# Scaling the attention values and taking some weight remainders on GpSimd, shifting three tiles' bits on VectorE, and moving one rounding forward

## The chip, the cores and the metric

The kernel runs on one core of one Trainium2 chip. The metric is the device time of one execution in microseconds (us); lower is better. Before the change the median of three runs is 564.09 us (562.98 to 564.4).

## What is computed

A retention layer (attention with a decaying state) over 2 batches of 8 heads, 768 positions and 64 channels, then two dense blocks on the 1536 x 512 result. Cut to what matters:

```
for t in range(S):                                   # retention, per batch and head
    state = gamma * state + outer(k[t], v[t])
    y[t] = scale * q[t] @ state
x = y as (1536, 512)
h = x @ w_in   (512 x 2048);  x = softplus(h) @ w_out        (2048 x 512)
h = x @ w2_in;                x = (h * clip(h + 3, 0, 6) / 6) @ w2_out
```

q, k and v are 32-bit numbers. The weights of both blocks reach the kernel as 64-bit numbers, two 32-bit words each, and the kernel itself turns them into 32-bit numbers.

## The kernel before, in words

**Names.** TensorE is PE, VectorE is DVE, ScalarE is ACT, GpSimd is POOL, SyncE is SP. A *unit* is 128 positions of one batch: there are 12, numbered 0 to 11. Units 0 to 3 make the first 512 rows of x and are the *head* of the kernel; units 4 to 11 are worked in pairs between the matmuls of the first dense block. A *weight tile* of the first block is 128 x 512 numbers: in0 to in15 from w_in, out0 to out15 from w_out. They are made in the order in0, in1, in2, out0, in3, out1, in4, out2, ... and numbered 0 to 31 in that order.

**Precision.** Each dense product is done three times in a rounded float32 form: high x high, high x low, low x high. So each weight tile, and each activation, is split: ACT copies it to the rounded *high* part, and the remainder, value minus high, is the *low* part.

**A weight tile** goes through these steps (class Words and weight()): SP loads its words into a `raw` buffer (five of them); ACT takes the top three bits of the low word (`bits`) and the sign (`sign`) into a `cv` buffer; the high word is scaled and clamped (`scale` on ACT and `clamp` on DVE, or `scaled` and `capped` on DVE); DVE joins them (`merge`); ACT rounds to the high part (`high`); DVE subtracts for the low part (`low`). For five tiles of the 32 the low part is made another way: ACT writes the negative and a DMA issued by POOL adds the value to it.

**A unit** loads k, q and v, turns k and q on PE (`ident` in the rows), scales q (`qT`) and v (`vs`) on DVE by powers of the decay, and multiplies: the scores, the masked scores with `vs`, and the state update with `vs`. In the head, the unit's result is rounded by ACT (`x_hi`) and the remainder is taken by DVE (`x_lo`). PE's first dense matmul needs `x_hi` of all four head units.

**The order.** Nothing is scheduled at run time. A planner (class Plan) holds every task with its engine, a cost, the tasks it follows and a due time, and hands out tasks greedily; the order in which it hands them out is each engine's program. Within a small window (NEAR) the task with the earliest due time goes first; a task with `ahead` set may be taken that much before it is ready. So a change of one task's engine or cost can re-order all engines. A GEMM block G1(f) is 12 matmuls of 128 x 512 with weight tile in f, G2(f) the same with out f on the softplus of G1(f)'s result.

**Pools.** `g2` holds five buffers for values that are read back from memory for the last 512 rows of the first block.

Of the kernel before, what the change touches and what calls it, by code (L numbers as in the profile page):

```python
# [10 lines left out]
F32 = mybir.dt.float32  # L11
F32R = mybir.dt.float32r
# [4 lines left out]
ALU = mybir.AluOpType  # L17
PSUM = bass.MemoryType.PSUM
P = 128
# [119 lines left out]
PSX, TT, TS, ACP, ACS = 0.61, 0.62, 0.36, 0.49, 0.55  # L139
# [6 lines left out]
def kernel(ctx, tc, q, k, v, w1_in, w1_out, w2_in, w2_out, table, out):  # L146
    nc = Plan(tc)
# [8 lines left out]
    CH = 512  # L156
    NC = NT // CH
    START = CH // C
    NU = B * NCH
    LAG = 2  # L160
    EARLY = 3
# [13 lines left out]
    def BY_DVE(n):  # L175
        return n < 10 or n < 2 * NF and n % 4 != 0
# [3 lines left out]
    def BY_ACT(n):  # L180
        return n < 4 or n >= 16

    def DIRECT(n):
        return True

# [16 lines left out]
    hold = holds.enter_context(tc.tile_pool(name="hold", bufs=1))  # L202

    def room(name, n, shape, dtype, within=None, later=()):
        nc.pool(name, n, later)
        slots[name] = {i: (within or fixed).tile(shape, dtype, name=f"{name}_{i}") for i in range(n)}
        kinds[name] = shape, dtype

    def at_slot(key):
        name, i = nc.slot[key]  # L210
        if name == "bank":
            return banks[:, i, :]
        if i not in slots[name]:
            slots[name][i] = late_p.tile(*kinds[name], name=f"{name}_{i}")
        return slots[name][i]
# [28 lines left out]
    room("g", 3, [P, CH], F32)  # L244
    room("hi", 2, [P, CH], F32R)
    room("lo", 3, [P, CH], F32R)
    for name, n, shape, dtype in (("sums", 1, [P, 4, CH // 2], F32), ("wf", 1, [P, 2, CH], F32), ("xl", 7, [P, 2, 2, CH], F32R), ("hs", 3, [P, CH], F32), ("g2", 5, [P, CH], F32), ("hi2", 7, [P, CH], F32R), ("lo2", 7, [P, CH], F32R),
                                  ("basel", 4, [P, CH], F32), ("partl", 2, [P, CH], F32), ("totall", 1, [P, CH], F32), ("xf", 7, [P, 2, 2, QT], F32R), ("keep", START + 2, [P, CH], F32), ("tf0", 2, [P, 2, QT], F32), ("tf1", 2, [P, 2, QT], F32), ("tf2", 2, [P, 2, QT], F32),
                                  ("base", 1, [P, QT], F32), ("part", 2, [P, QT], F32), ("total", 1, [P, QT], F32),
                                  ("c", 2, [P, 2, QT], F32), ("ob", 4, [P, CH], F32), ("e2", 2, [P, 2, QT], F32), ("parts", 3, [P, 2, 2, QT], F32R)):  # L250
        nc.pool(name, n)
        slots[name], kinds[name] = {}, (shape, dtype)
# [45 lines left out]
    n = 0  # L298
# [25 lines left out]
    for i in range(len(STEPS)):  # L324
        for name, n in PRODUCTS.items():
            n = min(n, 1) if i == 0 else n
# [10 lines left out]
    begin = -100.0  # L337
# [4 lines left out]
    def w_part(key, i):  # L342
        return at_slot(("w", key))[:, i]
# [7 lines left out]
    class Words:  # L351
# [26 lines left out]
        def bits(self):  # L378
            nc.scalar.activation(self.w(), self.raw()[:, :, 0], AF.Relu, scale=2.0 ** -29 * (1 - 2.0 ** -12), bias=half)

        def sign(self):
            nc.scalar.activation(self.w().bitcast(F16).rearrange("p (n x) -> p n x", x=2)[:, :, 1], self.y().bitcast(I32), AF.Copy, scale=2.0 ** -100)

# [12 lines left out]
        def merge(self):  # L396
            nc.vector.scalar_tensor_tensor(self.w(), self.y(), 3, self.w(), ALU.logical_shift_left, ALU.bitwise_or)

        def made(self, at, fetch_at, load, give, by_act=False, hold=0.0):
            T["F", self.key] = t0 = nc.add("SP", 0.45, self.fetch, due=fetch_at, take=[(f"raw{self.m}", self.raw_k)], load=load, hold=hold)  # L400
            t1 = nc.add("ACT", 0.65, self.bits, [t0], at - 3.5, take=[(f"cv{self.m}", self.cv_k)])
            if self.m or by_act:
                t4 = nc.add("ACT", SIGN, self.sign, [t1], at - 3.3)
                t2 = nc.add("ACT", 0.57, self.scale, [t4], at - 2.6)
                t3 = nc.add("DVE", TS, self.clamp, [t2], at - 2.0)
            else:
                t4 = nc.add("ACT", SIGN, self.sign, [t1], at - 2.9)
                t3 = nc.add("DVE", TS, self.scaled, [t0, t4], at - 2.7)
                t3 = nc.add("DVE", TS, self.capped, [t3], at - 2.3)
            return nc.add("DVE", TT, self.merge, [t3, t4], at - 1.3, give=give)  # L410

    def weight(o, f, number):
        key = 0, o, f
        x = Words(0, key, words[0][o])
        use = due[("G2" if o else "G1"), f] - 4.0
        made = second

        def high():
            nc.scalar.activation(w_part(key, 0), x.w().bitcast(F32), AF.Copy)

        def negative():
            nc.scalar.activation(w_part(key, 1), x.w().bitcast(F32), AF.Copy, scale=-1.0)

        def low():
            nc.vector.tensor_tensor(w_part(key, 1), x.w().bitcast(F32), w_part(key, 0).bitcast(F32), ALU.subtract)

        def add():
            nc.gpsimd.dma_start(out=w_part(key, 1).bitcast(F32), in_=x.w().bitcast(F32), accum_op=ALU.add)

        part = [("w", ("w", key))]  # L430
        tail = 1.5 if BY_DVE(number) else 7.0
        t5 = x.made(use - tail, begin + 15 if number < 1 else use - tail - 8.0, 1.45 if o else 1.5 if number < EARLY else 1.75, [x.raw_k], BY_ACT(number))
        if BY_DVE(number):
            a = nc.add("ACT", ACS, high, [t5], use - 1.5, take=part, give=[x.cv_k] + made)
            b = nc.add("DVE", TT, low, [a], use - 0.7, give=[x.cv_k] + made)
        else:
            n = nc.add("ACT", ACS, negative, [t5], use - tail, take=part)
            b = nc.add("POOL", 0.9, add, [n], use - tail + 1, give=[x.cv_k] + made, load=1.6)
            a = nc.add("ACT", ACS, high, [n], use - 2.5, give=[x.cv_k] + made)
        T["W", key] = [a, b]  # L440
        if not o:
            home = homes["in", f] = kept(f"words_in{f}", CH)
            T["S", key] = nc.add("SP", 0.45, lambda: nc.sync.dma_start(out=home, in_=x.w().bitcast(F32)), [t5], use, give=[x.cv_k] + made, load=0.8)
        elif o and f >= KEPT:
            home = kept(f"parts_out{f}")
            c = nc.add("SP", 0.45, lambda: nc.sync.dma_start(out=home, in_=at_slot(("w", key)).rearrange("p a n -> p (a n)").bitcast(F32)), [a, b], use + 8.0,
                       give=[("w", key)], load=1.6)
            for c_of in range(1 + (f in STAY), 3):
                back(("wl", c_of, f), home, c, due["G2", c_of * NF + f] - 8.0, 2.0)
# [4 lines left out]
    def kept(name, n=2 * CH):  # L454
        return stash.tile([P, n], F32, name=name)
# [19 lines left out]
    def back(key, home, after, when, lead=10.0):  # L475
        T["W", key] = [nc.add("SP", 0.45, lambda: nc.sync.dma_start(out=at_slot(key).rearrange("p a n -> p (a n)").bitcast(F32), in_=home),
                              [after], when, take=[("w", key)], load=1.6, hold=HOLD + when - lead)]
# [75 lines left out]
    for i, key in enumerate(order):  # L553
        weight(*key[1:], i)
# [64 lines left out]
    def attend(u):  # L619
        b, i = divmod(u, NCH)  # L620
# [5 lines left out]
        def task(eng, cost, fn, after, when, take=(), give=(), load=0.0, hold=0.0):  # L626
            when -= EDGE * (u < START and eng in ("DVE", "ACT"))
            return nc.add(eng, cost, fn, after, when, [(p, k) for p, k in take], list(give) + mine, load, hold)

        def tile_of(n):  # L630
            return at_slot((n, u))

        def own(n):
            return [(f"{n}{ph}", (n, u))]
# [17 lines left out]
        if u < START:  # L652
            at = [begin + 10 * u, begin + 10 * u + 1, begin + 10 * u + 3]
        else:
            at = [d["Tk"] - 11.0 + x / 2 for x in range(3)]
# [21 lines left out]
        sc, ds, o = ([(n, j, u) for j in range(2)] for n in ("sc", "ds", "o"))  # L677
        S, E = ("S", "D") if u < START else ("SS", "DD")
        kt, qt = [], []
        for x in range(parts):  # L680
            at = x and 0.1
            tp = task("PE", cost["Tk"] / parts, turned("k", x), [ik[x], ready.get(("S", u - 2))], d["Tk"] + at, take=[] if x else [("bank", ("kP", u))])
            kt.append(task("ACT", ACP if parts == 1 else act(NP * C // parts, True), lambda x=x: nc.scalar.activation(tile_of("kT")[:, ps(x)], bank(("kP", u))[:, ps(x)], AF.Copy), [tp], d[S] - 1.0 + at,
                           take=[] if x else own("kT"), give=[("kP", u)]))
            tp = task("PE", cost["Tq"] / parts, turned("q", x), [iq[x], ready.get(("C", u - 2))], d["Tq"] + at, take=[] if x else [("bank", ("qP", u))], give=[("q", u)])
            qt.append(task("DVE", PSX if parts == 1 else dve(NP * C // parts), lambda x=x: nc.vector.tensor_tensor(tile_of("qT")[:, ps(x)], bank(("qP", u))[:, ps(x)], tq_sb[:, ps(x)], ALU.mult), [tp, ready["q"]],
                           d[S] - 1.1 + at, take=[] if x else own("qT"), give=[("qP", u)]))
        vs = task("DVE", TT, lambda: nc.vector.tensor_tensor(
            tile_of("vs"), tile_of("v"), tk_sb.rearrange("p (h o) -> p h o", o=1).to_broadcast([P, H, HALF]), ALU.mult),
            [iv, ready["t"]], d[E] - 1.2, take=own("vs"), give=[("v", u)])  # L690
        if u >= START:
# [58 lines left out]
        if first:  # L750
            ready["end", u] = task("DVE", 0.42, faded, [dp, ready["t"]], (due["C", u + 1] if u + 1 < START else due["CC", u + 1]) - 2.0, take=[end], give=[end[1], dk])
            n = None
        else:
# [3 lines left out]
            n = task("DVE", 0.1, between, [c], d["C"] + 0.5)  # L757
        c = task("PE", cost["I0"], inner, pt + [vs, n], d["I"], take=[("bank", y) for y in o] if first else [],
                 give=[("pw", u), ("vs", u)])
        def x_at(part):  # L760
# [3 lines left out]
        o2 = task("ACT", PSX, lambda: nc.scalar.activation(x_at("hi"), split_out(), AF.Copy), [c], need - 1.5, give=o)  # L764
        o3 = task("DVE", PSX, lambda: nc.vector.tensor_tensor(x_at("lo"), split_out(), x_at("hi").bitcast(F32), ALU.subtract), [o2],
                  need - 0.8, give=o)
        ready["x", u] = [o2, o3]

    def pair(u, task):
# [479 lines left out]
```

## Time and profile before

| what | before |
|---|---|
| median of three runs | 564.09 us |
| the profiled execution's own time | 565.54 us |
| its span, first to last instruction | 563.4 us |
| granted TensorE clock | 1.0 of full speed throughout |
| PE busy | 554.1 us (98%) |
| DVE busy | 443.2 us (79%) |
| ACT busy | 365.3 us (65%) |
| POOL busy | 5.6 us (1%) |

The span is one execution by the hardware profiler; 2.1 us of the execution's own time lie around it. Line numbers are of little use, since a helper (L45) records nearly every operation: rows are told apart by engine and tile names, `output<-inputs`. Ends of matmuls are modelled, so a stall of PE shows best as a longer step between the starts of two matmuls.

### The profile page before, as it was taken

The page shows a single profiled execution, that of the slowest core. Times are in us where ns is not written, and L with a number is a line of the kernel's source. Part 1 is how long each engine was busy: PE and PEld are TensorE (multiplying, and loading weights), DVE is VectorE, ACT ScalarE, POOL GpSimd, SP SyncE. Part 2 cuts the span into 40 slices and gives each one's busy share as a digit, 9 for nine tenths or more (in the row PEclk, how much of TensorE's full clock was granted, in tenths as well). Part 3 has the DMA queues.
Part 4 walks back from the last instruction along what each step waited for, and adds up shares of the span by engine and source line. Part 5 has one row for each costly group of instructions (what it writes and reads, how often), then busy time and mean ns, then how long its engine had stood idle before and what let it go on. Part 6 is the DMA issues. An engine that isn't in the chain of part 4 may idle for free.

```text
span 563.4 us, 9586 instructions
## 1 busy us (share of the span) xinstructions
PE 554.1 (98%) x3679; PEld 473.3 (84%) x3679; DVE 443.2 (79%) x797; ACT 365.3 (65%) x604; POOL 5.6 (1%) x13
## 2 busy tenths in 40 slices
PE   8899999999999999999999999999999999999996
PEld 6688888787788888878888999988988899988895
DVE  4999998889989689989996885847787888854443
ACT  3598999998864445777957944448688685432220
POOL 0000000000000000000000000000000000000000
PEclk9999999999999999999999999999999999999999
DMA  9996999994423224846928522252655742236003
GB/s 204 282 247 244 284 281 290 340 281 165 139 64 105 94 77 152 276 169 224 328 88 293 187 74 76 74 188 76 229 212 194 269 180 76 75 100 237 1 0 113
DMA packets 80541, 98.41 MB, mean 175 GB/s; under 512 B 41328, under 2 KB 57968, under 8 KB 80496
## 3 DMA queue, kind: packets, MB, share of 16 engines
q1 hardware_dynamic: 79488, 96.35, 52.9%
q0 software_dynamic: 720, 1.31, 1.3%
q8 instruction: 29, 0.48, 0.4%
q10 hardware_dynamic: 288, 0.14, 0.1%
q14 instruction: 16, 0.13, 0.1%
HBM read 72.36 MB, written 24.12 MB: 171 GB/s over the span
## 4 chain that ended last, share of the span: by engine, by line
PE 74%; DVE 8%; ACT 7%; DMA 5%; issue 4%; POOL 0%; DVEq 0%; POOLq 0%; ACTq 0%; SPq 0%
PE banks L45 74%; ACT cv L45 3%; DMA w<-cv 1%; DMA raw<-in_moe_w_out_dram 1%; DVE w L45 1%; DVE raw L45 1%; ACT w L45 1%; DMA g<-stash_h 1%; DVE qT L45 1%; ACT raw L45 1%; DMA wf<-words_in 1%; DVE st L45 1%; DVE g L45 1%; DVE lo L45 1%; DVE cv L45 1%
## 5 line engine op out<-in xcount | busy, mean ns | idle before, releaser
L45 PE MATMUL banks<-w,parts 128*128 128x512 f32 x579 | 136.7, 390 | 0.0
L45 PEld LDWEIGHTS banks<-w,parts 128*128 128x128 f32 x579 | 108.1, 188 | 21.2
L45 PE MATMUL banks<-hi,w 128*128 128x512 f32 x384 | 125.1, 394 | 0.0
L45 PE MATMUL banks<-xf,w 128*128 128x384 f32 x672 | 123.6, 337 | 0.0
L45 PEld LDWEIGHTS banks<-xf,w 128*128 128x128 f32 x672 | 118.2, 188 | 3.5 <-DVE part L45 0.3
L45 PEld LDWEIGHTS banks<-hi,w 128*128 128x128 f32 x384 | 72.1, 188 | 15.1
L45 PE MATMUL banks<-xl,w 128*128 128x512 f32 x336 | 79.9, 392 | 0.2
L45 PE MATMUL banks<-lo,w 128*128 128x512 f32 x192 | 75.0, 391 | 0.0
L45 PEld LDWEIGHTS banks<-xl,w 128*128 128x128 f32 x336 | 62.6, 188 | 14.4 <-DVE hs L45 1.0
L45 ACT ACTIVATE cv<-raw,half 128x512 uint32<-128x512 uint32 x64 | 48.5, 759 | 14.0 <-DMA raw<-in_moe_w_in_dram 9.8
L45 ACT ACTIVATE e<-c,three 128x384 f32<-128x384 f32 (+1 forms) x32 | 24.7, 771 | 46.5 <-DVE c L45 45.9
L45 ACT ACTIVATE cv<-raw 128x512 f16<-128x512 int32 x64 | 50.0, 788 | 1.3
L45 DVE SCALAR_TENSOR_TENSOR cv<-raw,cv 128x512 uint32<-128x512 uint32 x64 | 43.9, 690 | 1.3
L45 PE MATMUL banks<-x_hi,w 128*128 128x512 f32 x128 | 42.8, 401 | 1.2 <-ACT x_hi L45 1.0
L45 DVE TENSOR_SCALAR raw<-raw 128x512 f32<-128x512 f32 x76 | 32.2, 428 | 14.4 <-ACT raw L45 13.6
L45 PEld LDWEIGHTS banks<-lo,w 128*128 128x128 f32 x192 | 36.1, 188 | 7.2 <-DVE lo L45 0.2
L45 ACT ACTIVATE e<-e 128x512 f32<-128x512 f32 x48 | 29.8, 626 | 14.1 <-DVE e L45 14.1
L45 DVE TENSOR_TENSOR parts<-c,parts 128x768 fp32r<-128x768 f32 x32 | 30.7, 958 | 9.3 <-ACT parts L45 8.7
L45 ACT ACTIVATE parts<-c 128x768 fp32r<-128x768 f32 x32 | 26.9, 841 | 16.1 <-DVE c L45 16.0
L45 DVE TENSOR_TENSOR lo<-g,hi 128x512 fp32r<-128x512 f32 x48 | 32.9, 687 | 5.2 <-ACT hi L45 4.9
L45 ACT ACTIVATE hi<-g 128x512 fp32r<-128x512 f32 x48 | 30.0, 626 | 10.0 <-DVE g L45 6.7
L45 DVE TENSOR_TENSOR c<-total,banks 128x384 f32<-128x384 f32 x16 | 8.9, 554 | 34.8 <-PE banks L45 34.7
(94 smaller groups left out, 686.2 us busy)
## 6 DMA issues: line engine op xcount, KB each, us to landing
raw<-in_moe_w_in_dram SPq DMA_DIRECT2D x32, 512.0 KB, 5.6
raw<-in_moe_w_out_dram SPq DMA_DIRECT2D x32, 512.0 KB, 6.0
w<-stash_out SPq DMA_DIRECT2D x32, 512.0 KB, 4.8
stash_out<-raw SPq DMA_DIRECT2D x16, 512.0 KB, 3.6
words_in<-cv SPq DMA_DIRECT2D x16, 256.0 KB, 6.5
parts_out<-w SPq DMA_DIRECT2D x8, 512.0 KB, 5.1
wf<-words_in SPq DMA_DIRECT2D x16, 256.0 KB, 2.8
stash_h<-hs SPq DMA_DIRECT2D x16, 256.0 KB, 2.0
```

The lines of the kernel that those rows point to most:

```text
L45: return self.plan.tc.keep_in_program_order(getattr(self.engine, op)(*args, **kwargs))
```

## The change

Four edits and one buffer count. (1) `vs` of units 1 to 11 is given to POOL. (2) The low part of weight tiles 2 to 7 (in2, out0, in3, out1, in4, out2) is given to POOL. (3) The three bits of tiles 3 to 5 (out0, in3, out1) are made by a shift on DVE in place of ACT's `bits`. (4) `x_hi` of unit 3 may be taken 1.5 us ahead of its time, so that ACT does it before other work. `g2` has four buffers where it had five.

```
+    def SHIFTED(n):
+        return 3 <= n < 6
...
-("g2", 5, [P, CH], F32)
+("g2", 4, [P, CH], F32)
...
+        def shifted(self):
+            nc.vector.tensor_scalar(self.w(), self.raw()[:, :, 0], 29, None, ALU.logical_shift_right)
...
-            t1 = nc.add("ACT", 0.65, self.bits, [t0], at - 3.5, take=[(f"cv{self.m}", self.cv_k)])
+            t1 = nc.add(*(("DVE", TS, self.shifted) if shifted else ("ACT", 0.65, self.bits)), [t0], at - 3.5, take=[(f"cv{self.m}", self.cv_k)])
...
-            b = nc.add("DVE", TT, low, [a], use - 0.7, give=[x.cv_k] + made)
+            by_pool = 2 <= number < 8
+            b = nc.add("POOL" if by_pool else "DVE", 1.45 if by_pool else TT, lambda: low(nc.gpsimd if by_pool else nc.vector), [a], use - (1.5 if by_pool else 0.7), give=[x.cv_k] + made)
...
-        vs = task("DVE", TT, lambda: nc.vector.tensor_tensor(
+        by_pool = u >= 1
+        vs = task("POOL" if by_pool else "DVE", 1.45 if by_pool else TT, lambda: (nc.gpsimd if by_pool else nc.vector).tensor_tensor(
...
+        if u == START - 1:
+            o2.ahead = 1.5
```

The planner then writes another program. Three places of it follow.

ACT at the end of the head (`x_hi` is unit 3's rounding; `cv_2`, `cv_3` and `cv_0` are the word buffers of in2, out0 and in3; a row with `half` is `bits`, one without is `sign`; `w_78` to `w_80` are the high parts of in1, in2 and out0), before:

```order
L45 ACTIVATE cv_2_75<-raw_2_70,half 128x512
L45 ACTIVATE cv_2_75<-raw_2_70 128x512
L45 ACTIVATE x_hi_299<-banks 128x4x128
L45 ACTIVATE w_78<-cv_1_74 128x512
L45 ACTIVATE raw_2_70<-raw_2_70 128x512
L45 ACTIVATE cv_3_76<-raw_3_71,half 128x512
L45 ACTIVATE cv_3_76<-raw_3_71 128x512
L45 ACTIVATE w_79<-cv_2_75 128x512
```

and now:

```order
L45 ACTIVATE cv_2_75<-raw_2_70,half 128x512
L45 ACTIVATE x_hi_299<-banks 128x4x128
L45 ACTIVATE w_78<-cv_1_74 128x512
L45 ACTIVATE cv_2_75<-raw_2_70 128x512
L45 ACTIVATE raw_2_70<-raw_2_70 128x512
L45 ACTIVATE cv_3_76<-raw_3_71 128x512
L45 ACTIVATE raw_3_71<-raw_3_71 128x512
L45 ACTIVATE w_79<-cv_2_75 128x512
```

One `sign` moved behind the rounding, and out0's `bits` is gone. Between `x_hi` and the first `hi` of the softplus chain ACT had 14 operations and now has 12.

PE at its fourth GEMM block (`w_81` is in3, `w_80` is out0, `w_79` is in2; `hi_94` and `lo_96` are the softplus of G1(0)), before:

```order
L45 MATMUL banks<-x_lo_311,w_81 128x512
L45 MATMUL banks<-x_hi_299,w_81 128x512
L45 MATMUL banks<-ident,k_1_140 128x128 x4
L45 MATMUL banks<-hi_94,w_80 128x512
L45 MATMUL banks<-lo_96,w_80 128x512
```

and now:

```order
L45 MATMUL banks<-x_lo_303,w_79 128x512
L45 MATMUL banks<-x_hi_299,w_79 128x512
L45 MATMUL banks<-hi_94,w_80 128x512
L45 MATMUL banks<-lo_96,w_80 128x512
```

G2(0) stood behind G1(3) and the turning of unit 5's k; now it follows G1(2) at once, and behind it stand both turnings of unit 5 (k, then q) and then G1(3).

POOL, whose program held five DMA issues there (the rows with `w` are low parts, those with `vs` the scaled values; the rows that begin with DMA add up a low part):

```order
+L45 TENSOR_TENSOR vs_1_150<-v_3_154,small 128x512
+L45 TENSOR_TENSOR w_79<-cv_2_75,w_79 128x512
+L45 TENSOR_TENSOR w_80<-cv_3_76,w_80 128x512
+L45 TENSOR_TENSOR w_81<-cv_0_73,w_81 128x512
+L45 TENSOR_TENSOR vs_0_149<-v_0_142,small 128x512
+L45 TENSOR_TENSOR w_82<-cv_3_76,w_82 128x512
+L45 TENSOR_TENSOR vs_1_150<-v_1_143,small 128x512
+L45 TENSOR_TENSOR w_83<-cv_1_74,w_83 128x512
+L45 TENSOR_TENSOR w_84<-cv_3_76,w_84 128x512
 L45 DMA w_88<-cv_1_74 128x512
```

Seventeen operations come into POOL's program: eleven `vs` and six low parts. Eight of them stand between the third `vs` and the first DMA issue. The last of the five DMA issues, for in15, stands right behind the fourth, and the last two `vs` come after it. On PE the block G1(15), which uses in15, now stands behind the scores of units 10 and 11 (32 short matmuls); before, those stood behind it.

## Rows read from the trace of the kernel before

**Rows 1.** Windows: busy us (x count) of PE, PEld, DVE, ACT, POOL; clock, DMA, GB/s.

```profile
28.00:60.00 32.00, 32.00 (x365) 25.68 (x365) 30.47 (x61) 29.52 (x50) 0.00 (x0) 1.00 0.84 248
88.00:121.00 33.00, 33.00 (x488) 26.54 (x487) 28.37 (x54) 32.62 (x57) 2.61 (x3) 1.00 1.05 308
```

**Rows 2.** Chain that ended last: start us, us, what.

```profile
120.05 8.40 DMA w<-cv
...
128.49 18.03 PE banks L45 x295
...
252.71 302.96 PE banks L45 x1479
```

**Rows 3.** Timeline of PE around the end of that DMA: start us, us, engine.

```profile
34.56 0.39 PE L45 MATMUL banks<-x_lo,w 128*128 128x512 f32 x1
34.79 0.40 PE L45 MATMUL banks<-x_hi,w 128*128 128x512 f32 x1
...
127.96 0.40 PE L45 MATMUL banks<-x_lo,w 128*128 128x512 f32 x1
128.49 0.73 PE L45 MATMUL banks<-x_hi,w 128*128 128x512 f32 x2
```

**Rows 4.** Timeline at the end of the head.

```profile
25.75 1.09 PE L45 MATMUL banks<-pw,vs 128*64 128x128 f32 x16 [0.38 <-DVE seen L45]
...
26.62 0.78 ACT L45 ACTIVATE cv<-raw 128x512 f16<-128x512 int32 x1
...
27.26 0.57 ACT L45 ACTIVATE x_hi<-banks 128x512 fp32r<-128x512 f32 x1
...
27.88 2.11 PE L45 MATMUL banks<-x_hi,w 128*128 128x512 f32 x8 [1.03 <-ACT x_hi L45]
```

**Rows 5.** Groups by shape: busy us, mean ns of one, idle before.

```profile
L45 DVE TENSOR_TENSOR vs<-v,small 128x512 f32<-128x512 f32 x12 | 8.2, 685 | 0.0
L45 DVE TENSOR_SCALAR raw<-raw 128x512 f32<-128x512 f32 x76 | 32.2, 428 | 14.4 <-ACT raw L45 13.6 <-ACT cv L45 0.4
L45 ACT ACTIVATE cv<-raw,half 128x512 uint32<-128x512 uint32 x64 | 48.5, 759 | 14.0 <-DMA raw<-in_moe_w_in_dram 9.8 <-DMA raw<-in_moe_w_out_dram 3.9
```

**Rows 6.** Timeline of POOL: its largest operation on tiles before the change.

```profile
1.37 0.28 POOL masks.py:66 TENSOR_SCALAR_AFFINE_SELECT small<-small 128x128 f32<-128x128 f32 x1
```

**Rows 7.** Timeline in the head: unit 1's v loaded, scaled, and used.

```profile
5.88 0.54 SPq L45 DMA_DIRECT2D v<-in_v_dram  x1
...
12.97 0.68 DVE L45 TENSOR_TENSOR vs<-v,small 128x512 f32<-128x512 f32 x1
...
14.89 0.69 PE L45 MATMUL banks<-vs,k 128*64 128x64 f32 x16
```

**Rows 8.** Timeline from G1(2) to G2(1): the softplus chain and unit 5.

```profile
34.25 0.48 PE L45 MATMUL banks<-x_hi,w 128*128 128x512 f32 x1
...
36.18 0.64 ACT L45 ACTIVATE hi<-g 128x512 fp32r<-128x512 f32 x1
...
37.00 0.69 DVE L45 TENSOR_TENSOR lo<-g,hi 128x512 fp32r<-128x512 f32 x1
...
39.88 0.66 PE L45 MATMUL banks<-ident,k 128*128 128x128 f32 x4
...
40.29 0.48 PE L45 MATMUL banks<-hi,w 128*128 128x512 f32 x1
40.32 1.06 ACT L45 ACTIVATE kT<-banks 128x512 f32<-128x512 f32 x2
...
43.12 0.60 PE L45 MATMUL banks<-ident,q 128*128 128x128 f32 x4
```

**Rows 9.** Timeline of the read-back values: first low part done, fifth buffer filled.

```profile
250.76 0.69 DVE L45 TENSOR_TENSOR lo<-g,hi 128x512 fp32r<-128x512 f32 x1
...
253.10 0.88 SPq L45 DMA_DIRECT2D g<-stash_h  x2
```

**Rows 10.** Waits of PE's weight loads over the whole run: total us, times, longest.

```profile
PEld banks L45 <- DVE hs L45: 1.0, 2, 0.5
```

More of the change, by code (lines that the diff above doesn't have):

```diff
@@ L246 @@
     room("lo", 3, [P, CH], F32R)
-    for name, n, shape, dtype in (("sums", 1, [P, 4, CH // 2], F32), ("wf", 1, [P, 2, CH], F32), ("xl", 7, [P, 2, 2, CH], F32R), ("hs", 3, [P, CH], F32), ("g2", 5, [P, CH], F32), ("hi2", 7, [P, CH], F32R), ("lo2", 7, [P, CH], F32R),
+    for name, n, shape, dtype in (("sums", 1, [P, 4, CH // 2], F32), ("wf", 1, [P, 2, CH], F32), ("xl", 7, [P, 2, 2, CH], F32R), ("hs", 3, [P, CH], F32), ("g2", 4, [P, CH], F32), ("hi2", 7, [P, CH], F32R), ("lo2", 7, [P, CH], F32R),
                                   ("basel", 4, [P, CH], F32), ("partl", 2, [P, CH], F32), ("totall", 1, [P, CH], F32), ("xf", 7, [P, 2, 2, QT], F32R), ("keep", START + 2, [P, CH], F32), ("tf0", 2, [P, 2, QT], F32), ("tf1", 2, [P, 2, QT], F32), ("tf2", 2, [P, 2, QT], F32),
@@ L397, in merge, with made @@
             nc.vector.scalar_tensor_tensor(self.w(), self.y(), 3, self.w(), ALU.logical_shift_left, ALU.bitwise_or)
-        def made(self, at, fetch_at, load, give, by_act=False, hold=0.0):
+        def made(self, at, fetch_at, load, give, by_act=False, hold=0.0, shifted=False):
             T["F", self.key] = t0 = nc.add("SP", 0.45, self.fetch, due=fetch_at, take=[(f"raw{self.m}", self.raw_k)], load=load, hold=hold)
-            t1 = nc.add("ACT", 0.65, self.bits, [t0], at - 3.5, take=[(f"cv{self.m}", self.cv_k)])
+            t1 = nc.add(*(("DVE", TS, self.shifted) if shifted else ("ACT", 0.65, self.bits)), [t0], at - 3.5, take=[(f"cv{self.m}", self.cv_k)])
             if self.m or by_act:
@@ L422, in negative, with low @@
             nc.scalar.activation(w_part(key, 1), x.w().bitcast(F32), AF.Copy, scale=-1.0)
-        def low():
-            nc.vector.tensor_tensor(w_part(key, 1), x.w().bitcast(F32), w_part(key, 0).bitcast(F32), ALU.subtract)
+        def low(by):
+            by.tensor_tensor(w_part(key, 1), x.w().bitcast(F32), w_part(key, 0).bitcast(F32), ALU.subtract)
         def add():
@@ L431, in weight @@
         tail = 1.5 if BY_DVE(number) else 7.0
-        t5 = x.made(use - tail, begin + 15 if number < 1 else use - tail - 8.0, 1.45 if o else 1.5 if number < EARLY else 1.75, [x.raw_k], BY_ACT(number))
+        t5 = x.made(use - tail, begin + 15 if number < 1 else use - tail - 8.0, 1.45 if o else 1.5 if number < EARLY else 1.75, [x.raw_k], BY_ACT(number), shifted=SHIFTED(number))
         if BY_DVE(number):
             a = nc.add("ACT", ACS, high, [t5], use - 1.5, take=part, give=[x.cv_k] + made)
-            b = nc.add("DVE", TT, low, [a], use - 0.7, give=[x.cv_k] + made)
+            by_pool = 2 <= number < 8
+            b = nc.add("POOL" if by_pool else "DVE", 1.45 if by_pool else TT, lambda: low(nc.gpsimd if by_pool else nc.vector), [a], use - (1.5 if by_pool else 0.7), give=[x.cv_k] + made)
         else:
```

## The prediction, on record before the changed kernel ran

> **What bounds the kernel now.** I read three views: the busy time by stage, the chain that ended last, and the timeline at the places where that chain leaves PE. From 28 us on PE is busy all the time, 32.00 of 32 us and 33.00 of 33 us in the stages shown; DVE and ACT are nearly as full there, 30.47 and 29.52 of 32 us between 28 and 60 us, and ACT has 32.62 of 33 us between 88 and 121 us, with the DMA engines at 1.05 [rows 1]. So PE sets the pace, and the other two just keep up. The chain agrees: it is PE alone from 128.49 us to the end, but for short waits, the last long piece being 302.96 us from 252.71 us on [rows 2]. Before 128.49 us it hangs on the DMA that adds up in15's low part, issued at 120.05 us and landed 8.40 us later. PE's own loss there is small: from the matmul at 127.96 us to the next it takes 0.53 us, where the same step takes 0.23 us elsewhere [rows 3]. So what this change can win is the time until PE's first dense matmul at 27.88 us [rows 4] and a few waits of some tenths; what it can lose is any new wait of PE after that, one for one. PE's work itself stays the same.
>
> **The head (edit 4).** Unit 3's last matmuls start at 25.75 us and take 1.09 us, so they end at 26.84 us. ACT is then in `sign`, from 26.62 us, and `x_hi` starts at 27.26 us; PE follows at 27.88 us, 0.62 us later [rows 4]. With the `sign` moved behind, ACT is free by 26.62 us and `x_hi` starts when the matmuls end, which I put at 26.88 us. PE starts at 27.50 us. **Term: -0.38 us.** It costs a `sign` that is 0.57 us later; `x_hi` and ACT's three lost operations pay for that at once, below.
>
> **What moves between engines.** DVE loses eleven `vs` and six low parts, all two-input instructions over 128x512 as the `vs` row, 17 x 0.685 = 11.6 us, and gains three shifts. A shift of 128x512 was not traced on DVE; between the clamp on the same buffers with the same stride, 0.428 us, and the two-input form, 0.685 us, it is nearest to the clamp, so 0.43 us each, 1.3 us in all. ACT loses three `bits` at 0.759 us, 2.3 us [rows 5]. POOL gains 17 operations of two inputs over 512 columns. None was traced. POOL's nearest row reads one input of 128 columns in 0.28 us [rows 6]: four times the columns give 1.12 us, twice the inputs 2.24 us as the upper bound, and DVE's 0.685 us for the same shape [rows 5] is the lower one. I take 1.1 us, the row of POOL's own. [...]
>
> **What POOL's results are waited for.** Unit 1's `vs`: v is issued at 5.88 us and is there by 12.97 us at the latest, since DVE starts on it then; PE needs it at 14.89 us [rows 7]. At 1.1 us it is done by 14.1 us; at 2.24 us it would be 0.3 us late. Cost nothing, covered by PE's scores before it; units 2 and 3 have their values earlier still against PE. The low parts queue up on POOL in the order in2, out0, in3, `vs` 4, out1, and PE wants them in blocks of 2.8 us (from 40.29 to 43.12 us [rows 8]), each first at the block's third matmul. One POOL operation per block fits twice. Behind a `vs` that waits for its v, the next low part waits too; the pairs' `vs` are needed a block or more after their scores, so I cost this at nothing; if that cover is gone, one POOL operation, 1.1 us, is late.
>
> **The softplus chain, where it gets tight.** G2(0) stood behind G1(3) and started at 40.29 us; `hi` was made at 36.18 us and `lo` ended at 37.69 us, so it had 2.6 us to spare [rows 8]. Now it stands right behind G1(2), which started at 34.25 us and moves to 33.87 us: G2(0) wants `hi` at 36.7 us and `lo` at 36.9 us. ACT has two operations fewer before `hi` (three `bits` gone, one `sign` added, 1.5 us) and started 0.38 us earlier: `hi` from 34.3 us if ACT stays full, to 34.9 us by my walk with DVE's queue, ending at 35.5 us; `lo` ends at 36.2 us. So 0.7 us to spare, and no wait if POOL and DVE do not hinder each other.
>
> Right behind G2(0), at about 39.5 us, come unit 5's turnings of k and q, 0.41 us each, and each needs one of the two banks that unit 4's turnings hold until `kT` (ACT) and `qT` (DVE) have read them. `kT` started at 40.32 us before; with the same operations ahead of it, less what ACT gained and plus one `hi` that passed it, it starts at 39.3 to 40.3 us and ends 0.5 us on. PE would want that bank at 39.9 us. The wait is 0 to 0.9 us; I take 0.2 us, since the walk's early end gives none. The wait for the bank at 39.88 us, 0.1 us, goes. **Term: +0.1 us.**
>
> **In15.** ACT has fewer operations before in15's negative, and PE has the scores of units 10 and 11 to do before G1(15). Either is worth more than the 0.30 us that PE lost there [rows 3]: 32 short matmuls alone take over 0.3 us. **Term: -0.30 us.**
>
> **Four read-back buffers.** The fifth buffer was filled from 253.10 us on, after the first buffer's low part had ended at 251.44 us [rows 9]. So the fifth load finds the first buffer free, and PE's G2 blocks of these rows start later still. Cost nothing; cover: 1.7 us at the first re-use.
>
> **The sum.** -0.38 + 0.1 - 0.30 = -0.58 us. On the profiled execution's 565.54 us (a span of 563.4 us and 2.1 us around it) that gives 564.96 us; that execution was 1.45 us above the median, so on the median of 564.09 us **563.5 us**. Its own range, by the bounds above, is 562.9 to 564.7 us.
>
> **Rivals.**
>
> *POOL and DVE take turns (slower).* If a POOL operation on tiles stops DVE, or DVE stops it, then each move costs DVE 1.1 us in place of 0.685 us. The place is 31 to 37 us: in2's, out0's and in3's low parts fall among the DVE operations that lead to `lo`. Three times 1.1 us less the 0.7 us to spare is a wait of 2.6 us at G2(0). Over 28 to 60 us DVE had 30.47 of 32 us [rows 1]; less eight moved operations (5.5 us), plus three shifts (1.3 us) and eight stops (8.8 us) it would need 35.1 us, 3.1 us too much. So +2.6 to +3.1 us: 563.5 + 2.85 = **566.3 us**. It decides from a stop of about 0.25 us per POOL operation on, where the spare is used up. Nothing in the trace before speaks for or against it: POOL works on tiles only in the first 2 us. [...] Against its full price: `qT`, the masks, the states' sums and `x_lo` read one input from the banks, and a POOL operation that waits for DVE loses little, as its results are early. Chance 0.26, of which 0.05 with a price too small to leave the 0.3%.
>
> *Nothing remains.* The new order gives back elsewhere what it wins: PE's blocks were re-ordered between 34 and 160 us, and a new wait of 0.6 us, say the whole 0.9 us for the bank, uses it up: **564.1 us**. Chance 0.17.
>
> *More waits go (faster).* DVE is 10.3 us and ACT 2.3 us lighter where both were full. PE's weight loads, which run ahead of its matmuls, waited twice for `hs`, 1.0 us in all [rows 10]; the second wait ends where the chain enters PE at 252.71 us [rows 2]. If these two go, and two smaller ones of the size of the 0.30 us at in15, half of them seen at the matmuls, and the wait for the bank does not come, that is 1.0 + 0.3 + 0.2 = 1.5 us more: **562.0 us**. Against it: both waits for `hs` lie in stages that the edits do not reach. Chance 0.17.
>
> **The numbers.** Forecast 0.40. What a measurement of this kernel can tell from no change is about 0.3%, 1.7 us: below 562.4 us or above 565.8 us. Faster holds most of the last rival and a little of the forecast, 0.2; slower most of the first, 0.22; the rest, 0.58, is the same. The range for 8 in 10 takes in the last rival's 562.0 us and the first one's 566.3 us: **562.0 to 566.3 us**.
>
> **What would show it.** Right: PE's first dense matmul near 27.5 us; POOL's operations near 1.1 us; DVE's operations as long as before while POOL works; `lo` of G2(0) done before PE ends G1(2); no step of 0.53 us at in15. Wrong: `raw`, `cv` or `lo` operations on DVE stretched to 1 us or more between 31 and 58 us and PE idle at about 37 us (the first rival); a wait of PE at the turning of unit 5's q (the second). A POOL operation of 2 us or more would make the forecast wrong at both places.

## The result, and the profile after

| | before | after |
|---|---|---|
| median | 564.40 us (562.98 to 565.21, five runs) | 571.13 us (570.87 to 572.78, five runs) |
| profiled span | 563.4 us | 569.4 us |
| ratio of the times | | 1.0133, 95% interval 1.0115 to 1.0151 |

The change makes the kernel 6.7 us slower, outside the range of 562.0 to 566.3 us that was given. The first lines to read are the busy times and two lines of the 40 slices on the page of the changed kernel:
```profile
PE 554.8 (97%) x3679; PEld 473.5 (83%) x3679; DVE 448.0 (79%) x783; ACT 364.4 (64%) x601; POOL 25.4 (4%) x30
...
POOL 1142011110000000000000000000000000000000
PEclk9989999999999999999999999999999999999999
```
POOL has 17 instructions and 19.8 us more. DVE has 14 instructions fewer (17 out, three in), and yet it is busy *longer*, 448.0 us against 443.2 us. The third slice of the clock is below full speed. The window says where (its columns are those of [rows 1]):
```profile
28.00:60.00 32.00, 28.06 (x217) 21.95 (x216) 29.86 (x45) 22.22 (x38) 10.27 (x8) 0.89 0.75 216
```
Against [rows 1], DVE is as full as before between 28 and 60 us but gets through 45 instructions in place of 61; ACT, which waits for it, is 7 us emptier, and PE loses 3.9 us and some clock. From 88 to 121 us PE loses 0.36 us alone. So the loss lies between 28 and 60 us. The groups by shape of DVE and POOL (busy us, mean ns) show which instructions grew:
```profile
L45 DVE TENSOR_SCALAR raw<-raw 128x512 f32<-128x512 f32 x76 | 35.4, 469 | 10.9 <-ACT raw L45 9.8 <-ACT cv L45 0.8
...
L45 DVE TENSOR_SCALAR e<-g 128x512 uint32<-128x512 uint32 x48 | 24.2, 507 | 2.0 <-DMA g<-stash_h 0.9 <-ACT g L45 0.8
...
L45 DVE TENSOR_TENSOR qT<-banks,tq_sb 128x512 f32<-128x512 f32 x11 | 7.5, 684 | 1.8 <-PE banks L45 1.6
```
```profile
L45 POOL TENSOR_TENSOR vs<-v,small 128x512 f32<-128x512 f32 x11 | 12.5, 1139 | 41.1 <-DMA v<-in_v_dram 39.5 <-PE banks L45 1.6
L45 POOL TENSOR_TENSOR w<-cv,w 128x512 fp32r<-128x512 f32 x6 | 7.9, 1318 | 23.7 <-ACT w L45 23.7
```
`raw<-raw` (the clamp) has a mean of 469 ns against 428 ns in [rows 5], while `qT`, which reads the banks, stays at 684 ns. A mean hides what happens; the timelines show it. First POOL, then DVE, in the same stretch:
```profile
31.14 1.48 POOL L45 TENSOR_TENSOR w<-cv,w 128x512 fp32r<-128x512 f32 x1 [10.84 <-ACT w L45]
32.78 1.29 POOL L45 TENSOR_TENSOR w<-cv,w 128x512 fp32r<-128x512 f32 x1 [0.16 <-ACT w L45]
36.34 1.28 POOL L45 TENSOR_TENSOR w<-cv,w 128x512 fp32r<-128x512 f32 x1 [2.27 <-ACT w L45]
37.58 1.22 POOL L45 TENSOR_TENSOR vs<-v,small 128x512 f32<-128x512 f32 x1
```
```profile
30.77 0.69 DVE L45 SCALAR_TENSOR_TENSOR cv<-raw,cv 128x512 uint32<-128x512 uint32 x1
31.58 1.32 DVE L45 TENSOR_SCALAR e<-g 128x512 uint32<-128x512 uint32 x1
32.82 1.99 DVE L45 TENSOR_SCALAR raw<-raw 128x512 f32<-128x512 f32 x2
...
36.40 1.50 DVE L45 TENSOR_SCALAR e<-g 128x512 uint32<-128x512 uint32 x1
37.83 1.52 DVE L45 TENSOR_TENSOR lo<-g,hi 128x512 fp32r<-128x512 f32 x1
```
A DVE row that begins while POOL is at work ends a little less than its own length after POOL's: POOL ends at 32.62 us, `e<-g` (0.42 us long before) at 32.90 us; POOL ends at 37.62 us, `e<-g` at 37.90 us; POOL ends at 38.80 us, `lo` (0.69 us) at 39.35 us. DVE stood still and then did its work. POOL waits too: its row of 31.14 us overlaps DVE's `merge` until 31.46 us and takes 1.48 us, where the next two low parts take 1.29 and 1.28 us. Between 28 and 60 us eight such encounters make DVE's rows 7.5 us longer than the same forms were before (0.42, 0.43 and 0.69 us). PE's timeline shows who waits:
```profile
35.65 0.39 PE L45 MATMUL banks<-x_hi,w 128*128 128x512 f32 x1
36.86 0.51 PE L45 MATMUL banks<-hi,w 128*128 128x512 f32 x1 [0.82 <-ACT hi L45]
39.41 0.79 PE L45 MATMUL banks<-lo,w 128*128 128x512 f32 x1 [2.04 <-DVE lo L45]
40.00 1.05 PE L45 MATMUL banks<-hi,w 128*128 128x512 f32 x2
...
44.26 1.05 PE L45 MATMUL banks<-ident,k 128*128 128x128 f32 x4
...
53.40 1.15 PE L45 MATMUL banks<-vs,k 64*64 64x64 f32 x48 [0.81 <-DVE pw L45]
```
G2(0)'s first two steps are 0.98 and 2.32 us longer than usual. Behind that idle time each step is 0.43 us in place of 0.23 us, and the windows show the granted clock of these stretches, 0.80 and then 0.50:
```profile
36.00:40.00 4.00, 1.14 (x4) 0.69 (x3) 3.97 (x6) 3.25 (x6) 2.46 (x2) 0.80 1.10 288
40.00:44.00 4.00, 4.00 (x11) 3.13 (x10) 3.96 (x6) 2.90 (x5) 2.32 (x2) 0.50 0.93 284
```
The account from PE's first dense matmul to the end of the span: 543.3 us after (569.4 - 26.08) against 535.5 us (563.4 - 27.88), 7.8 us more. Four longer steps between 28 and 60 us make 0.43 + 0.98 + 2.32 + 0.88 = 4.6 us; the eleven matmuls from 39.41 to 44.26 us take 4.85 us in place of 11 x 0.23 = 2.53 us, 2.3 us by the clock. That is 6.9 us of the 7.8; the rest are steps longer by about half a microsecond further on. One of them, at 104.69 us, waits for DVE's `qT`, and `qT` came late behind a low part on DVE that took 1.43 us (from 102.60 us) beside a `vs` on POOL (from 102.44 us): one more stop of the same kind.

The head, which answers to [rows 4]:
```profile
24.06 1.09 PE L45 MATMUL banks<-pw,vs 128*64 128x128 f32 x16 [0.36 <-DVE seen L45]
...
24.78 0.77 ACT L45 ACTIVATE cv<-raw,half 128x512 uint32<-128x512 uint32 x1
...
25.45 0.58 ACT L45 ACTIVATE x_hi<-banks 128x512 fp32r<-128x512 f32 x1
26.08 2.11 PE L45 MATMUL banks<-x_hi,w 128*128 128x512 f32 x8 [0.92 <-ACT x_hi L45]
...
27.03 0.43 DVE L45 TENSOR_SCALAR cv<-raw 128x512 uint32<-128x512 uint32 x1 [0.97 <-DMA raw<-in_moe_w_out_dram]
...
27.71 0.68 DVE L45 TENSOR_TENSOR x_lo<-banks,x_hi 128x512 fp32r<-128x512 f32 x1
...
28.45 1.21 PE L45 MATMUL banks<-x_lo,w 128*128 128x512 f32 x4 [0.27 <-DVE x_lo L45]
```
From unit 3's last matmuls to PE's first dense one it takes 2.02 us; in [rows 4] it was 2.13 us. ACT was still in in2's `bits` when the matmuls ended, so only 0.11 us of the 0.38 us came. And the first shift waited 0.97 us on DVE for its words to land; behind it `x_lo` was late, the 0.43 us at 28.45 us. Both belong to this one execution, whose head ran early. Two of the runs below, e4 and e7, have the changed kernel's program up to G2(0): in their profiles the step is 1.79 us, the shift does not wait, and `x_lo` is in time.

### The profile page after: what moved, and what is told of

Read it like the earlier page. It is cut to its first block, busy times and chain, and to the rows that moved or that the text cites. A ratio compares the mean times of both kernels' runs of the same rounds, so it can differ in the third digit from the quotient of the medians.

```text
span 569.4 us, 9607 instructions
## 1 busy us (share of the span) xinstructions
PE 554.8 (97%) x3679; PEld 473.5 (83%) x3679; DVE 448.0 (79%) x783; ACT 364.4 (64%) x601; POOL 25.4 (4%) x30
## 4 chain that ended last, share of the span: by engine, by line
PE 70%; DVE 11%; ACT 7%; DMA 7%; SPq 2%; issue 2%; DVEq 0%; ACTq 0%
PE banks L45 70%; ACT cv L45 3%; SPq L45 2%; DMA raw<-in_moe_w_out_dram 2%; DVE raw L45 2%; DVE g L45 2%; DMA v<-in_v_dram 1%; DVE lo L45 1%; ACT w L45 1%; DVE cv L45 1%; DMA g<-stash_h 1%; DVE w L45 1%; DMA stash_out<-raw 1%; DVE st L45 1%; DVE e L45 1%
## 5 line engine op out<-in xcount | busy, mean ns | idle before, releaser
L45 ACT ACTIVATE cv<-raw,half 128x512 uint32<-128x512 uint32 x61 | 46.1, 758 | 10.2 <-DMA raw<-in_moe_w_out_dram 5.9
L45 DVE TENSOR_SCALAR raw<-raw 128x512 f32<-128x512 f32 x76 | 35.4, 469 | 10.9 <-ACT raw L45 9.8
```

The source lines that it names most:

```text
L45: return self.plan.tc.keep_in_program_order(getattr(self.engine, op)(*args, **kwargs))
```

## The experiments

All ratios are to the kernel before, run beside them on the same chip (its medians there: 564.11, 564.25 and 564.50 us for the first, second and third four). There are two theories: *taking turns* (POOL's and DVE's work on tiles shut each other out) and *order* (the plan written for a lighter DVE is what costs).

**Engine alone, order of before** (e1):
```
-nc.vector.tensor_tensor(w_part(key, 1), ...          # low(), plan unchanged
+(nc.gpsimd if 2 <= number < 8 else nc.vector).tensor_tensor(w_part(key, 1), ...
-vs = task("DVE", TT, lambda: nc.vector.tensor_tensor(
+vs = task("DVE", TT, lambda: (nc.gpsimd if u >= 1 else nc.vector).tensor_tensor(
```


> The program of before, PE's and ACT's order unchanged row for row; the eleven `vs` and the six low parts stand where they stood but are issued to POOL. Taking turns (POOL's and DVE's operations on tiles shut each other out): `clamp`, `merge` and low-part operations on DVE that lie beside a POOL operation grow from 0.43 to 0.69 us to 1.2 to 1.7 us; G2(0) has its 2.6 us of spare here, which takes two or three such stops, so PE waits 0 to 1 us there and the kernel takes 564.5 to 567 us. Order (the new order of PE's blocks took the spare, and the engine matters little): DVE is 11.6 us lighter and nothing else has changed, 563 to 564.5 us, no wait at G2(0).

Measured: 567.14 us, ratio 1.0054 (1.0036 to 1.0073). Slower by 3.0 us, just above the 564.5 to 567 us that taking turns gave; *order* alone would have had it the same as before. No PE, ACT or SP row moved, and DVE only lost rows. Over the whole program DVE's grown means add 9.8 us to its rows, less than the 11.6 us that were moved away; so it is not a larger total on DVE that makes this run slower. The wait at G2(0)'s `lo` stayed away, as its 2.6 us of spare said, but others came, one of them for a low part on POOL itself, which took 1.29 us there:
```profile
36.71 0.73 PE L45 MATMUL banks<-x_hi,w 128*128 128x512 f32 x2 [0.58 <-POOL w L45]
```

**Order alone** (e2): the changed kernel's plan, the 17 operations issued to DVE.
```
-lambda: low(nc.gpsimd if by_pool else nc.vector)
+lambda: low(nc.vector)
-(nc.gpsimd if by_pool else nc.vector).tensor_tensor(
+nc.vector.tensor_tensor(
```


> The changed kernel's program, PE's and ACT's order unchanged row for row; the seventeen operations stay where its plan puts them but are issued to DVE, so POOL works on no tile. Taking turns: the stretched operations are gone, `lo` of G2(0) is done at about 37 us again, PE waits there less than 0.5 us, the granted clock stays at 1.0; 563 to 565.5 us. Order: G2(0) right behind G1(2) is too early whatever makes the low parts, PE waits over 1.5 us there and the kernel takes 567 to 571 us.

Measured: 568.65 us, ratio 1.0082 (1.0055 to 1.011). Between the two theories: no row is stretched (the clamps have a mean of 425 ns, the low parts 686 ns) and the wait at G2(0) is 0.7 us, but PE waits at unit 5's turnings and for `pw` (1.19 us, not shown):
```profile
36.71 0.50 PE L45 MATMUL banks<-lo,w 128*128 128x512 f32 x1 [0.51 <-DVE lo L45]
...
39.91 0.66 PE L45 MATMUL banks<-ident,k 128*128 128x128 f32 x4 [0.42 <-DVE qT L45]
41.06 0.66 PE L45 MATMUL banks<-ident,q 128*128 128x128 f32 x4 [0.49 <-ACT kT L45]
```
So an order that counts on a lighter DVE costs 4.5 us if DVE is not lighter. It does not say that PE's early order is at fault: here the 17 rows also stand in DVE's queue where the plan thought POOL had them.

**No moves to POOL** (e3): `by_pool = False` at both places, planned so.

> The changed kernel without the two moves to POOL: the three shifts on DVE, the earlier rounding and four read-back buffers stay. Taking turns and order both: 563.5 to 564.5 us, PE's first dense matmul at 27.5 us or earlier. Other edits (the shift that waits on DVE for its words to land holds DVE's queue and makes the softplus late): 566 us or more, a step of PE over 1 us between 28 and 40 us.

Measured: 564.68 us, ratio 1.0009 (0.999 to 1.0027): no difference. PE's order is the early one here too, G2(0) right behind G1(2) and both turnings behind it, and the step at G2(0)'s `lo` is 0.16 us longer, no more. So the early order does no harm where DVE's own plan knows its load. The shifts, the earlier rounding and the four buffers together cost nothing that can be seen.

**`lo` last in G2(0)** (e4):
```
-for n, (l, r) in enumerate(((wh, hi), (wh, lo), (wl, hi))):
+for n, (l, r) in enumerate(((wh, hi), (wl, hi)) if s == 0 else ((wh, hi), (wh, lo), (wl, hi))):
...
+for j in js if s == 0 else ():
+    nc.tensor.matmul(at_slot(("acc", c, j)), wh[:, j * P:(j + 1) * P], lo, start=False, stop=False)
```


> The changed kernel, but G2(0) does its eight matmuls with `hi` first and its four with `lo` last, so that `lo` is wanted 7 x 0.23 = 1.6 us later; all else stands. If the loss is one late `lo` and the lower clock behind it: of the wait of 2.3 us 0.7 us or less stay, the granted clock stays at 1.0 behind it and gives back another 2.2 us: 567 to 568 us. If DVE is simply too slow from 28 to 60 us, the lateness comes out at the next block: 570 us or more, with new waits for DVE between 40 and 60 us.

Measured: 572.24 us, ratio 1.0157 (1.0115 to 1.0199). The wait shrank as wanted, and came out behind it. The granted clock is 0.95 between 28 and 60 us; it reads 1.00 from 36 to 44 us and from 52 to 60 us, and the steps before 36 us are 0.23 us, so it was low between 44 and 52 us, behind these waits:
```profile
39.94 1.20 PE L45 MATMUL banks<-lo,w 128*128 128x512 f32 x4 [0.45 <-DVE lo L45]
42.67 0.65 PE L45 MATMUL banks<-ident,k 128*128 128x128 f32 x4 [1.54 <-DVE qT L45]
```
That is the second case expected: giving one wait more room only moves it, as it would where DVE is too slow over the whole stretch.

**Eight subtractions beside the kernel before** (e5):
```
+if 2 <= number < 10:                                  # in low(), behind DVE's own
+    a = w_part(key, 0).bitcast(F32)
+    nc.gpsimd.tensor_tensor(spare[:, 0], a, a, ALU.subtract)
```


> The kernel before, with eight additional subtractions on POOL (128x512, both inputs the rounded high part of weight tiles 2 to 9, the result to a spare tile that nothing reads). Nothing waits for them, and no other engine's order changes. Taking turns: 1.05 us each on POOL, and each stretches one or two of DVE's `clamp`, `merge` or low-part operations by 0.5 to 1.0 us between 31 and 70 us; DVE is nearly full there, so PE's waits for DVE grow by 1 to 4 us and the kernel takes 565 to 568 us. If only the late results of POOL cost the time: 564 us, DVE's mean times as before (0.428 and 0.686 us).

Measured: 570.29 us, ratio 1.0101 (1.0076 to 1.0125), more than I had priced. Nothing is moved and no engine's order changes, so this is the price of the turns alone. The eight encounters make DVE's rows 6.1 us longer in the profile, and the kernel is 6.0 us slower (570.29 against 564.25 us). One of POOL's rows, then DVE's beside it:
```profile
34.02 1.22 POOL L45 TENSOR_TENSOR spare<-w 128x512 f32<-128x512 f32 x1 [1.83 <-ACT w L45]
```
```profile
34.26 1.53 DVE L45 TENSOR_TENSOR w<-cv,w 128x512 fp32r<-128x512 f32 x1
```

**Eight fills in their place** (e6):
```
-    nc.gpsimd.tensor_tensor(spare[:, 0], a, a, ALU.subtract)
+    nc.gpsimd.tensor_copy(spare[:, 0, :1], w_part(key, 0).bitcast(F32)[:, :1])
+    nc.gpsimd.memset(spare[:, 0], 0.0)
```


> As the run with eight subtractions beside the kernel before, but each subtraction is a one-column copy (so that it starts at the same place) and a fill of 128x512 numbers, which reads nothing. Taking turns on whole instructions whatever POOL does: DVE's operations are stretched beside the fills as well, 565 us or more. Taking turns only where POOL reads tiles: no operation of DVE with two inputs is stretched by more than 0.15 us, 564 us.

Measured: 564.90 us, ratio 1.0008 (0.9988 to 1.0028): no difference. The same group of DVE over the whole program with the subtractions, and then with the fills:
```profile
L45 DVE TENSOR_TENSOR w<-cv,w 128x512 fp32r<-128x512 f32 x35 | 26.5, 758 | 1.4 <-ACT w L45 1.4
```
```profile
L45 DVE TENSOR_TENSOR w<-cv,w 128x512 fp32r<-128x512 f32 x35 | 24.0, 685 | 1.4 <-ACT w L45 1.3
```
A fill takes 0.53 us on POOL against 1.04 us or more, so the fills are the smaller load as well; but the two-input rows did not grow beside them (between 28 and 70 us the means of their groups over 128x512 that read tiles alone are 678 to 687 ns; 686 to 690 ns in the kernel before). The size is not the reason. The one-column copies read a tile and are smaller still, 0.18 us alone; yet three of them, which met a two-input row of DVE near its start, took 0.64 to 0.73 us, while the fills beside such rows kept their 0.53 us. POOL's rows, then DVE's:
```profile
35.05 0.73 POOL L45 COPY spare<-w 128x1 f32<-128x1 f32 x1 [1.43 <-ACT w L45]
35.84 0.53 POOL L45 MEMSET spare<- 128x512 f32 x1
```
```profile
35.05 0.68 DVE L45 TENSOR_TENSOR w<-cv,w 128x512 fp32r<-128x512 f32 x1
35.66 0.68 DVE L45 TENSOR_TENSOR lo<-g,hi 128x512 fp32r<-128x512 f32 x1
```
Some of the clamps, which have one input, did grow beside fills: three took 1.64 us, where the same three take 1.23 us in the kernel before, with a fill on POOL in their midst:
```profile
54.91 1.64 DVE L45 TENSOR_SCALAR raw<-raw 128x512 f32<-128x512 f32 x3
```
```profile
55.09 0.70 POOL L45 MEMSET spare<- 128x512 f32 x1
```
So, between 28 and 70 us, both kinds are stretched beside the subtractions (the clamps have a mean of 555 ns against 432 ns in the kernel before, the low parts 917 ns against 687 ns), and beside the fills only one-input rows (the clamps 450 ns, the low parts 685 ns). Rows of VectorE that read the banks are not: in the changed kernel a `qT` took 0.69 us from 41.40 us on and a low part on POOL 1.28 us from 41.68 us on, and the mean of `qT` is 684 ns. Why a fill stretches the one kind and not the other no run here shows.

**Ten more matmuls in the wait** (e7), in the changed kernel:
```
+for x in range(10 if s == 0 else 0):
+    nc.tensor.matmul(at_slot(("acc", c, 0)), wh[:, :P], hi, start=True, stop=True)
```


> The changed kernel with ten additional matmuls of `hi` ahead of G2(0), whose result is written over: 10 x 0.23 = 2.3 us of work where PE waited 2.3 us for `lo`. If the idle time made the granted clock fall: the steps behind it stay at 0.23 us, the 2.2 us come back, the rest of the loss stays; 568.5 to 569.5 us. If the clock falls there for another reason: steps of 0.43 us as in the changed kernel, 571 us or more.

Measured: 572.78 us, ratio 1.0144 (1.0115 to 1.0172). Neither case: the clock stays up at G2(0) (1.00 between 36 and 44 us, and still from 44 to 52 us), and falls later, behind a longer wait for `pw`. PE's timeline and the window:
```profile
53.84 1.16 PE L45 MATMUL banks<-vs,k 64*64 64x64 f32 x48 [2.25 <-DVE pw L45]
...
55.33 0.63 PE L45 MATMUL banks<-x_lo,w 128*128 128x512 f32 x1
55.75 1.05 PE L45 MATMUL banks<-x_hi,w 128*128 128x512 f32 x2
```
```profile
52.00:60.00 8.00, 6.16 (x63) 5.06 (x64) 7.83 (x14) 5.93 (x10) 1.28 (x1) 0.79 0.51 162
```
In both e4 and e7 the lower clock stands behind idle time and goes where it goes, and the loss stays; this fits DVE's rate over the stretch setting the loss, which e5 shows by itself.

**The earlier rounding alone, by the planner** (e8): `o2.ahead = 1.5` and four `g2` buffers in the kernel before.

> The kernel before with the earlier rounding of unit 3 and four read-back buffers alone; PE's order is that of before. My term for the head: PE's first dense matmul 0.62 us less 0.38 us, that is 0.24 us, behind the end of unit 3's matmuls in place of 0.62 us, and the later `sign` costs nothing: 563.7 us against 564.1 us, inside what can be measured. If the later `sign` or the other order of the word buffers costs as much: 564.1 us or more, with a new wait of PE between 28 and 40 us.

Measured: 565.85 us, ratio 1.0029 (1.0014 to 1.0045). Slower by 1.6 us, which I had not expected. PE's order is that of before but for one group of six matmuls near the end; ACT and DVE, though, are re-ordered by the planner in many places up to the end of the program. In the profile PE waits at a place 400 us behind the edit:
```profile
428.29 2.01 PE L45 MATMUL banks<-xf,w 128*128 128x384 f32 x10 [1.18 <-ACT base L45]
```

**The same row moved by hand** (e12): the `sign` of in2 is held back and issued behind in1's `high`; no other row of any engine moves.
```
...
+if t.tag == "held":          # the sign of in2
+    held = t.fn
+    continue
 t.fn()
+if t.tag == "then":          # in1's high, behind x_hi of unit 3
+    held()
...
```


> The program of before with one row moved by hand: the `sign` of in2 stands behind unit 3's rounding and in1's `high`, as the earlier rounding has it, and no other row of any engine moves. My term for the head: 0.24 us from the end of unit 3's matmuls to `x_hi` gone, 0.38 us in all; 563.9 us, inside what can be measured, and the step from unit 3's last matmuls to PE's first dense matmul 0.3 to 0.4 us shorter than in [rows 4]. If the earlier rounding is what made its run 1.6 us slower: 565.5 us. If the plan's other changes far behind it did: 564.2 us or less.

Measured: 564.50 us, ratio 1.0001 (0.9984 to 1.0018): no difference.
```profile
24.10 1.09 PE L45 MATMUL banks<-pw,vs 128*64 128x128 f32 x16 [0.38 <-DVE seen L45]
...
25.24 0.60 ACT L45 ACTIVATE x_hi<-banks 128x512 fp32r<-128x512 f32 x1 [0.32 <-PE banks L45]
...
25.89 2.11 PE L45 MATMUL banks<-x_hi,w 128*128 128x512 f32 x8 [0.70 <-ACT x_hi L45]
```
From unit 3's last matmuls to PE's first dense one: 1.79 us against 2.13 us in [rows 4], 0.34 us gained where 0.38 us was forecast. The 1.6 us of e8 therefore do not come from this row. The other rows that the planner moved are left, or the four read-back buffers, where e12 has five; but e3 has four as well and loses nothing. Which of the rows, beyond the one wait shown, stays open.

**POOL in the plan without POOL** (e9): the orders of e3, the 17 operations issued to POOL, edited as in e1.

> The program of the run without moves to POOL (it took 564.7 us; PE's and ACT's order stay as there, G2(0) right behind G1(2)), with the eleven `vs` and six low parts issued to POOL where they stand. Taking turns: G2(0) has no spare here, so every stop before it reaches PE; more than the 3.0 us that the same move cost in the order of before: 568 to 571 us, the wait at G2(0) over 1 us. If what the changed kernel lost beyond those 3.0 us came from the plan that counted on a free DVE: 566.5 to 567.8 us.

Measured: 569.55 us, ratio 1.0091 (1.0062 to 1.0121), 4.9 us above e3 and 5.1 us above the kernel before. That is as taking turns gave: without G2(0)'s spare the same move costs more than the 3.0 us of e1, though the two intervals overlap a little. To the changed kernel's 571.13 us some 1.6 us are left by the medians, and those intervals overlap too. The plan that counted on a free DVE may account for them, or the lower clock, which e9 does not have (1.00 between 28 and 60 us); no run tells the two apart. PE's row at G2(0), whose step is 1.1 us longer than usual:
```profile
37.24 0.50 PE L45 MATMUL banks<-lo,w 128*128 128x512 f32 x1 [0.86 <-DVE lo L45]
```

**The two moves apart** (e10: only `vs` on POOL; e11: only the low parts): `by_pool = False` at the other place.

> The changed kernel with the low parts back on DVE, in the plan too; the eleven `vs` stay on POOL. Taking turns, by place: three `vs` lie in the head, where DVE has gaps, two between 28 and 60 us and six behind 60 us, where DVE is 85 to 95% busy: 565 to 567 us. If the count of POOL's operations decides: eleven of seventeen, 568.5 us or more.

> The changed kernel with the `vs` back on DVE, in the plan too; the six low parts stay on POOL, all between 28 and 60 us where DVE is full. Taking turns, by place: most of the loss stays, 567 to 570 us. If the count decides: six of seventeen, 566.5 us or less.

Measured: `vs` alone 566.68 us, ratio 1.0046 (1.0031 to 1.0061); low parts alone 569.62 us, ratio 1.0091 (1.0062 to 1.0121). The place counts for more than the number, as expected: six operations where DVE is full cost 5.1 us, eleven that are spread out 2.2 us. (Each of the two has its own plan, and e8 shows that a new plan can cost 1.6 us by itself; the difference of 2.9 us is larger.) Between 28 and 60 us PE is busy for 31.13 of 32 us with `vs` alone (two of them lie there) and for 29.62 us with the low parts alone.

No version beats the kernel before. Three match it: e3 and e12, without POOL's work on tiles, and e6, whose work on POOL reads next to nothing.

## Why the prediction was wrong

- **The step that failed** is "So 0.7 us to spare, and no wait if POOL and DVE do not hinder each other". They do; the forecast put the hindrance at nothing, with no row to show it. Each of the eight POOL operations between 28 and 60 us took 0.94 us on the mean from DVE (7.5 us in all), so DVE lost more than it was relieved of: its grown means add 13.0 us over the program, while the moves take 11.6 us from it and the shifts give 1.3 us back. In e1 and e9 the grown means add less than the moves take, 9.8 and 9.3 us, and both are slower all the same: DVE's total does not decide it, which fits that a stop costs most ahead of a row that PE waits for (e10 and e11). This is the first rival, which I gave 0.26, and e5 and e6 show its mechanism by itself. "Nothing in the trace before speaks for or against it" was not quite so: at 60.48 us, beside a DMA issue on POOL, two clamps took 1.03 us together, where others take 0.89 us.
- **The rival's price was mis-sized**: 2.85 us above the forecast's 563.5 us, measured 7.6 us above it (6.7 us above the kernel before). Its terms were near: 1.1 us per stop (0.94), 2.6 us at G2(0) (0.98 + 2.32 = 3.3). What I left out is what came behind PE's idle time here: the granted clock fell to 0.50 and the steps took 2.3 us more, and with DVE short over the whole stretch a further wait came (`pw`, 0.88 us). I had priced the lateness where it first shows, and then once for the stretch, and not both.
- **The place and the signs** were right: stretched DVE rows between 31 and 58 us, PE idle at 37 us.
- **POOL's operation, 1.1 us**: right for a `vs` (six of the eleven took 1.04 or 1.05 us; the mean of 1.14 us contains four of 1.22 to 1.38 us). A low part, whose output is rounded, was mis-sized: the six of the changed kernel took 1.28 to 1.48 us. **The shift, 0.43 us**: 0.42 to 0.43 us. Its wait for the words, 0.97 us at 27.03 us, was not in the sum; e4 and e7 do not have it.
- **The head, -0.38 us**: right. It is 0.34 us where nothing else moves (e12) and the same in e4 and e7, where PE's first dense matmul starts at 27.55 and 27.61 us. In the profiled execution of the changed kernel it is 0.11 us, as ACT was still in in2's `bits`.
- **Unit 5's bank, +0.1 us**: no wait to be seen in the changed kernel, where PE came too late for it, and none in e3, which has the same order there; 1.3 us at the two turnings in e2, whose DVE is not lighter, past the bound of 0.9 us. **In15, -0.30 us**: right, no wait for that DMA is left. **Four buffers, nothing**: right by e3. **Unit 1's `vs` on POOL**: right, PE waits for no `vs`.

## What to carry to other kernels

Before work goes from VectorE to GpSimd to relieve it, ask what VectorE reads meanwhile: where both read tiles from SBUF a GpSimd operation here stopped VectorE for most of its own length (0.94 us on the mean of the eight between 28 and 60 us in the changed kernel, which took 1.22 to 1.48 us). An operation of 0.69 us moved away cost 0.76 us of stops on the mean in the changed kernel (13.0 us for 17), 0.94 us where VectorE was full, and 0.55 to 0.58 us in e9 and e1, which were slower too. No run shows the move paying; what room is left for it, by these rows, is beside VectorE's reads of the banks (the `qT` of 0.69 us) or in its idle time. A wait that makes TensorE idle can be followed by slower steps (2.3 us in the changed kernel; none in e9, which waited as well), and these belong into its price. And with a greedy planner even a one-row edit should be tried as one row moved by hand, since the plan's re-ordering can cost more than the edit gives.

## What the runs showed of the hardware beyond that

The head of one and the same program differs between executions by 1.7 us. The changed kernel and e4 have the same program up to G2(0), and unit 3's last matmuls start at 24.06 us in the one and at 25.76 us in the other; PE's rows of unit 1's k in the one and in the other:
```profile
8.31 0.66 PE L45 MATMUL banks<-ident,k 128*128 128x128 f32 x4
```
```profile
9.62 1.10 PE L45 MATMUL banks<-ident,k 128*128 128x128 f32 x4
```
In the second PE's steps are nearly twice as long here, though the clock column reads 1.00 in both; why stays open. It is the main reason that PE's first dense matmul lies at 26.08 us in the changed kernel and at 27.55 us in e4, and why the account above is taken from that matmul on.
